# Value products of a block-local attention over two key blocks and three query blocks at a time, in a fused attention and feed-forward kernel

## The chip, the cores and the metric

One core of one Trainium2 chip runs the whole program. The metric is the device time of one execution in microseconds (us), as the median of several runs. Beside it stands one profiled execution, whose trace gives the start and the length of every instruction on TensorE (PE), VectorE (DVE), ScalarE (ACT) and GpSimd (POOL) and the issue of every DMA.

## The reference

```python
# q, k, v: (8 batches, 8 heads, 576, 64), float32
scores = np.matmul(q, k.transpose(0, 1, 3, 2)) / 8
rel = pos[:, None] - pos[None, :]
mask_local = (rel >= 0) & (rel < 32)                                # heads 0 to 3
mask_strided = (rel >= 0) & (pos[None, :] % 32 == pos[:, None] % 32)   # heads 4 to 7
attn = softmax(where(mask, scores, -1e9))
x = (attn @ v).transpose(0, 2, 1, 3).reshape(4608, 512)
h = x @ w_in                                                        # (4608, 2048)
g = where(h >= 1, h, where(h <= -1, 0, (h + 1) ** 2 / 4))
out = g @ w_out                                                     # (4608, 512)
```

A query of a local head sees itself and the 31 keys before it. With blocks of 32 positions, a query block needs its own key block and the one before: 64 keys.

## The kernel before, in words

The kernel does the attention batch by batch and the two products of the feed-forward block, which are most of the work, around it. The order is written out by hand: `AGENDA` is a list of times, each with the names of the steps that are recorded there. `2j0` is step `j` of unit 0 of batch 2. Engines run their own instructions in that order; DMAs are issued almost all on SP's queue, also in that order, and a DMA that waits holds all that stand behind it on the queue. DMA completions are counted on eight semaphores in turn, which SP's queue and the few DMAs on ACT's queue share: a DMA is issued only when the one before it on its semaphore has landed.

Each batch has four units. Unit 0 is the first twelve query blocks of the four local heads, unit 1 the other six, units 2 and 3 are the strided heads. The steps of unit 0 that matter here:

- `s`, score (line 592): for each query block, 32 queries against 64 keys, of two heads at a time (64 rows of the array each).
- `m` and the letters that follow: mask, softmax, in `pr`, 128 x 768.
- `t`, turn (line 743): DVE transposes 32 x 32 squares, into two tiles `t`.
- `j`, spread (line 753): two DMAs of 192 KB write them to a DRAM tile `there`.
- `J`, gather (line 764): four DMAs of 96 KB read them back into `pT`, so that the 64 keys of a query block stand on 64 partitions.
- `F`, fetch_v (line 538): loads of `v`, 384 KB for six query blocks; rows of a key block that two query blocks share stand there twice.
- `v`, value (line 779): for each of 12 query blocks and 4 heads one product, 64 keys x 64 columns of v as the stationary operand and 32 queries as the moving one. Four of them (two halves of the rows, two of the columns) fill the array.

A float32 product shows as two records in the trace, so the 48 products of unit 0 are 96 records of form `64*64 64x32`. Unit 1 and the strided units use the same line with 64x32 and 54x64.

The feed-forward block reads its weights as a stream: `wr<-kq` and `wr<-ks` (line 971, 256 KB each) go through a ring of seven tiles; every group of six matmuls (1.36 us) uses one up. These loads stand on SP's queue between the attention's DMAs. In the early part of the program the weights come in as `raw` (line 436) and are converted on ACT and POOL.

Of the kernel before, what the change touches and what calls it, by code (L numbers as in the profile page):

```python
# [8 lines left out]
F32 = mybir.dt.float32  # L9
# [25 lines left out]
-53.5 L3.1  # L35
-52.5 1s1 1m1 B3.1
-51.845 L7.1 A2.1 B2.1 D4.0 E4.0
# [42 lines left out]
0.95 2s0 D10 2m0 S10  # L80
2.51 2x0 2b0 2e0 2F1 2s1
4.5 C11 N11 2Q2 R11
5.45 2q0 2k0 2w0 2t0 2j0
6.51 D11 S11
# [22 lines left out]
31.45 3a2 2F2  # L107
33.45 3p1 S12 3w1 3t1 2V1 3j0 4Q0
35.45 3e2 2h1 3q2 2h3 3j1 C01
# [6 lines left out]
41.45 3J0  # L116
42.5 4m0 4x0 C02 3F1
43.45 3J1 3v0 N02 4s1 O00
# [11 lines left out]
59.45 4Q2 4s2 G0s10 G0t30 G0p60 4e1 4q1 R04 S03 3F2  # L130
59.95 3J3 4m2 S00 4j0 4p1 3V1 3h3 3h1
61.45 G0p32 4w1 4t1 4x2
63.45 G0s11
64.5 Y05 4F1 D04 4F0 4a2 4e2 4J0
65.45 4j1 N05
# [23 lines left out]
115 G0s40  # L159
117 S07 5F1 5e0 5q0 5k0 G0p41 G0s41 X1.1 X1.-6 X1.-4  # L160
119 R01 D01 G0s42
121 X1.6 G0s43 G0r30 S01 X1.7 X1.-5 G0r31
123 G0r40 5w0 5t0 X1.5 5m2 5x2 5b2
125.5 X1.4 G0r41 5j0 X1.3
128.5 5e2 5q2 5p2 5r2
131.5 5t2 5j2
# [14 lines left out]
163.5 5F2 6a1 5J1  # L181
170.5 6e1 6q1 6p1 6r1 6s2 6m2 6x2 6b2 5V1 6F1
171.5 6j0
175.5 6t1 6J0
179.5 G1s12
181 6F0
# [25 lines left out]
247.5 7w1  # L212
248.5 7F1
249.5 7a0 7e0
# [4 lines left out]
259.5 7q0 7k0 7r0  # L219
263.5 7t0 7j0  # L220
266.5 G2s11
267.5 G2p61
# [66 lines left out]
def tile_sparse_attention_then_ffn(  # L289
# [4 lines left out]
    v_l: bass.AP,  # L294
    v_s: bass.AP,
    w: bass.AP,
    out: bass.AP,
# [34 lines left out]
    def slots(u):  # L332

        n, rest = divmod(UNITS[u][2], IL if UNITS[u][0] else IS)
        return n + (rest > 0), n
# [50 lines left out]
    for i in range(IL):  # L386
        part = slice(i * QL, (i + 1) * QL)
        for n0, n1, off in ((0, SLOTS, ST),) if i else ((0, 1, 0), (1, SLOTS, ST)):
            t = m_loc[part, n0:n1]
            nc.gpsimd.affine_select(out=t, in_=t, compare_op=ALU.is_ge, fill=NEG, base=off,  # L390
                                    pattern=[[0, n1 - n0], [-1, WL]], channel_multiplier=1)
            nc.gpsimd.affine_select(out=t, in_=t, compare_op=ALU.is_ge, fill=NEG, base=ST - 1 - off,
                                    pattern=[[0, n1 - n0], [1, WL]], channel_multiplier=-1)
    for i in range(IS):
# [23 lines left out]
    SUMS_AT = (("X1a", "X1b", "w0", "w1", "w0", "w1", "w0", "w1"), ("X0b", "X0a", "X0b", "X0a", "w11", "w12", "w13", "w14"))  # L418
    w_v = w.bitcast(U32).rearrange("f p (i e t) -> f p i e t", i=2, t=2)

    kept = [[(dram.tile([P, 3, 2, HF], F32, tag=f"kq{i}{j}", name=f"kq_{i}_{j}"),
# [106 lines left out]
    def load_v(b, u, k=None):  # L528

        local, b0, nb = UNITS[u]  # L530
        if k is not None:
            b0, nb = b0 + k * VB, min(VB, nb - k * VB)
        src = (v_l if local else v_s)[b][:, b0:b0 + nb]
        if b == 0 and u in (0, 3):
            t = place(5 if u else 4, list(src.shape), F32, f"v_{b}_{u}")
        else:
            t = v_p.tile([P, VB, 2, D], F32, tag="v", name=f"v_{b}_{u}_{k}")[:, :nb]
        nc.sync.dma_start(t, src)
        for n in range(nb):
            loaded[b, local, b0 + n] = t[:, n]  # L540
# [6 lines left out]
    def fetch_v(b, *parts):  # L547
        for u, k in parts:
            if 0 < b < B and (b, UNITS[u][0], UNITS[u][1] + k * VB) not in loaded:
                load_v(b, u, k)  # L550


    def attention(b, kinds):

        probs, flipped, there, ahead, covered = {}, {}, {}, {}, set()
# [23 lines left out]
        def score(u, pairs=range(2)):  # L579
            local, b0, nb = UNITS[u]  # L580
            Q, W, I, p0 = (QL, WL, IL, 0) if local else (QS, WS, IS, 2)
            if 0 in pairs:
                probs[u] = banks(u, "s"), W
            sc = probs[u][0]
            for p in pairs:
                for n in range(nb):
                    q0 = (b0 + n) * (QL if local else WS)
                    k0 = max(q0 - ST, 0) if local else q0
                    for j in range(2):
                        _, s, i = seat(u, n, j)  # L590
                        qk = loaded[b, p0 + p, "qk"][j * D:(j + 1) * D]
                        nc.tensor.matmul(sc[j][i * Q:(i + 1) * Q, s, p], qk[:, 0, q0:q0 + Q],  # L592
                                         qk[:, 1, k0:k0 + W], start=u not in covered,
                                         stop=u not in covered)
# [23 lines left out]
        def homes(u):  # L618
# [15 lines left out]
            if ns[0] > ns[1]:  # L634
                todo += [(j, slice(j * 64, j * 64 + 64), ns[1], ns[0], ns[1]) for j in range(2)]
            pieces_ = []
            for j, part, s0, s1, at in todo:
                of = part, slice(2 * at, 2 * (at + s1 - s0))
                pieces_.append((sc[j][part, s0:s1], pr[of].rearrange("p (n h) w -> p n h w", h=2), part, of[1]))
# [107 lines left out]
        def spread(u):  # L747

            ts = probs.pop(u)
            n = sum(slots(u))  # L750
            there[u] = to = dram.tile([P, 2, 2, n, ST], F32, tag=f"t{u}", name=f"there_{b}_{u}")
            for h in range(2):
                nc.sync.dma_start(to[:, h], ts[h][:, :, :n])

        def gather(u):

            n = sum(slots(u))
            pool, tag = (o_p, "ob") if u == 1 else (pt_p, "pT")
            pT = pool.tile([P, 4, n if u == 1 else 2 * SLOTS, ST], F32, tag=tag, name=f"pT_{b}_{u}")
            src = there.pop(u).rearrange("(i c) h k n q -> h k c i (n q)", c=ST)  # L760
            for h in range(2):
                for k in range(2):
                    at = h * 64 + k * ST
                    nc.sync.dma_start(pT[at:at + ST, :, :n].rearrange("p i n q -> p i (n q)"), src[h, k])
            flipped[u] = pT

        def value(u, xp=None):
            local, b0, nb = UNITS[u]
            Q = QL if local else QS
            pT = flipped.pop(u)  # L770
            xp = xp or banks(u, "v")
            for n in range(nb):
                K = WL if local else LAST if b0 + n == NB_S - 1 else WS
# [389 lines left out]
    with tc.manual_schedule():  # L1163
# [25 lines left out]
        def step(name):  # L1189
# [12 lines left out]
            elif kind in "UV":  # L1202
                up(0, int(kind == "V"), rest == "0", rest == "1")
            elif kind == "W":
                for i in range(2):
# [67 lines left out]
def _layout(q, k, v, moe_w_in, moe_w_out):  # L1273
# [18 lines left out]
    keys = np.arange(0, S, QL)  # L1292
    keys = np.maximum(keys - ST, 0)[:, None] + np.arange(WL)[None, :]

# [3 lines left out]

    v_l = by_key(v[:, :HL][:, :, keys])
    v_s = np.pad(by_class(v[:, HL:]), [(0, 0)] * 2 + [(0, NB * WS - S), (0, 0)]).reshape(B, HL, NB, WS, D)  # L1300
    v_s = by_key(np.pad(v_s, [(0, 0)] * 3 + [(0, 64 - WS), (0, 0)]))
# [3 lines left out]
    w = np.concatenate([w_in, w_out.reshape(DFF // P, P, DM)], 2)  # L1305
    return {"qk_l": qk_l, "qk_s": qk_s, "v_l": v_l, "v_s": v_s, "w": w}

# [19 lines left out]
```

## Time and profile before

| | |
|---|---|
| median of 3 runs | 801.52 us (801.34 to 803.21) |
| the profiled execution | 802.56 us |
| its span, first to last instruction | 800.8 us |
| PE busy | 792.0 us, 99% of the span |
| DVE, ACT, POOL busy | 618.5, 505.2, 260.0 us |
| mean granted TensorE clock | 1.000 of full speed |
| moved by DMA | 209.78 MB, mean 262 GB/s |

The span is what the trace shows; the execution's own time is 1.76 us longer, and the median of the runs is 1.04 us below the profiled execution. In the trace's rows "x96" is a count of records merged into one row; the length of such a row reaches to the modelled end of the last one, which lies inside the next row, since matmuls are pipelined. In the chain of waits the pieces do not overlap.

### The profile page before, as it was taken

The numbers are of one execution on the slowest core, as the hardware profiler recorded it, in microseconds if no ns is written. First come the engines' busy times: TensorE is split into PE (matmuls) and PEld (weight loads), VectorE is DVE, ScalarE is ACT, GpSimd is POOL, SyncE is SP. The second block draws the span as 40 slices with busy tenths as digits, with TensorE's granted clock in tenths as the row PEclk, the third lists the DMA queues.
The fourth block names the chain that finished last, engine by engine and source line by source line (L and its number), as shares of the span: only waits on it lengthen the run. The fifth ranks groups of instructions, "written<-read, shape, count | busy, mean of one in ns | idle before, by whom it ended". The sixth has DMA issues, their size and how long they took to land.

```text
span 800.8 us, 17840 instructions
## 1 busy us (share of the span) xinstructions
PE 792.0 (99%) x6921; PEld 647.6 (81%) x6921; DVE 618.5 (77%) x881; ACT 505.2 (63%) x857; POOL 260.0 (32%) x203
## 2 busy tenths in 40 slices
PE   8999999999999999999999999999999999999998
PEld 6778888888887887878888888888888888888886
DVE  5999879989989999878689786675786854566673
ACT  5899854566764556677665456677544667775442
POOL 5456345887483320022141102132424001224000
PEclk9999999999999999999999999999999999999999
DMA  9948788898899999888889778777777675666665
GB/s 344 407 195 300 296 294 307 286 327 281 291 308 309 295 312 349 276 283 272 260 248 298 240 222 260 255 233 213 213 253 245 212 241 191 195 195 189 217 203 166
DMA packets 107699, 209.78 MB, mean 262 GB/s; under 512 B 17760, under 2 KB 33376, under 8 KB 105568
## 3 DMA queue, kind: packets, MB, share of 16 engines
q1 hardware_dynamic: 100560, 179.15, 69.5%
q10 hardware_dynamic: 7056, 29.49, 9.5%
q8 instruction: 55, 0.90, 0.5%
q14 instruction: 28, 0.23, 0.1%
HBM read 161.94 MB, written 46.66 MB: 260 GB/s over the span
## 4 chain that ended last, share of the span: by engine, by line
PE 95%; DMA 2%; issue 1%; DVE 1%; ACT 1%; POOL 0%; SPq 0%; POOLq 0%
PE yo L1135 21%; PE h L887 16%; PE y L1040 16%; PE zo L1135 11%; PE z L1040 8%; PE o L947 6%; PE xo L1135 5%; PE x L1040 4%; PE xp L779 3%; PE sc L592 3%; DMA qk<-in_qk_l 1%; DMA wr<-kq 1%; PE sc L577 0%; PE tp L719 0%; DVE xq_b L850 0%
## 5 line engine op out<-in xcount | busy, mean ns | idle before, releaser
L1135 PE MATMUL yo<-hl,wr 128*128 128x512 f32 x768 | 177.6, 390 | 0.0
L1135 PEld LDWEIGHTS yo<-hl,wr 128*128 128x128 f32 x768 | 143.5, 188 | 30.9 <-DVE hl L997 0.9
L1040 PE MATMUL y<-x,wr 128*128 128x512 f32 x576 | 139.9, 389 | 0.0
L1040 PEld LDWEIGHTS y<-x,wr 128*128 128x128 f32 x576 | 108.0, 188 | 22.5
L887 PE MATMUL h<-xq_a,w 128*128 128x512 f32 x384 | 122.9, 394 | 0.0
L1096 POOL TENSOR_TENSOR ga<-gb,ga 128x1024 f32<-128x1024 f32 x17 | 44.1, 2601 | 236.3 <-DVE ga L897 175.5
L997 DVE TENSOR_TENSOR hl<-ga,hl 128x1024 fp32r<-128x1024 f32 x48 | 63.9, 1346 | 36.6 <-ACT hl L996 35.0
L1135 PE MATMUL zo<-hl,wr 128*128 128x512 f32 x384 | 89.4, 391 | 0.0
L887 PEld LDWEIGHTS h<-xq_a,w 128*128 128x128 f32 x384 | 72.0, 188 | 15.7
L1135 PEld LDWEIGHTS zo<-hl,wr 128*128 128x128 f32 x384 | 71.6, 188 | 15.8 <-DVE hl L997 0.6
L996 ACT CAST hl<-ga 128x1024 fp32r<-128x1024 f32 x48 | 50.0, 1052 | 51.1 <-PE yo L1135 16.3
L887 PE MATMUL h<-xq_b,w 128*128 128x512 f32 x192 | 73.6, 391 | 0.1
L1040 PE MATMUL z<-x,wr 128*128 128x512 f32 x288 | 73.5, 390 | 0.0
L1040 PEld LDWEIGHTS z<-x,wr 128*128 128x128 f32 x288 | 53.8, 188 | 11.3
L894 ACT ACTIVATE tmp<-tmp 128x512 f32<-128x512 f32 x96 | 60.9, 634 | 3.1
L997 DVE TENSOR_TENSOR hl<-gb,hl 128x1024 fp32r<-128x1024 f32 x36 | 48.7, 1367 | 14.4 <-ACT hl L996 14.3
L996 ACT CAST hl<-gb 128x1024 fp32r<-128x1024 f32 x36 | 37.8, 1057 | 31.2 <-PE zo L1135 15.2
L504 POOL TENSOR_TENSOR st<-st 128x256 f32<-128x256 f32 x48 | 50.7, 1059 | 14.0 <-DVE st L705 6.4
L897 DVE SCALAR_TENSOR_TENSOR ga<-ga,tmp 128x512 f32<-128x512 f32 x48 | 33.1, 689 | 28.3 <-ACT tmp L894 28.0
L891 ACT ACTIVATE u<-h,half 128x512 f32<-128x512 f32 x48 | 32.9, 686 | 30.2 <-PE h L887 21.2
L469 POOL TENSOR_TENSOR raw<-raw 128x512 uint32<-128x512 uint32 (+1 forms) x34 | 35.9, 1067 | 42.1 <-DVE raw L465 16.7
L682 POOL TENSOR_TENSOR pr<-pr,st 128x384 f32<-128x384 f32 (+3 forms) x18 | 26.7, 1487 | 63.8 <-DVE st L678 63.7
(124 smaller groups left out, 1409.1 us busy)
## 6 DMA issues: line engine op xcount, KB each, us to landing
wr<-ks SPq DMA_DIRECT2D x224, 256.0 KB, 4.0
wr<-kq SPq DMA_DIRECT2D x168, 256.0 KB, 3.4
ks<-st ACTq DMA_DIRECT2D x16, 1024.0 KB, 7.0
raw<-in_w SPq DMA_DIRECT2D x30, 512.0 KB, 9.7
qk<-in_qk_s SPq DMA_DIRECT2D x16, 604.0 KB, 6.9
qk<-in_qk_l SPq DMA_DIRECT2D x16, 576.0 KB, 6.7
kq<-w ACTq DMA_DIRECT2D x16, 512.0 KB, 3.8
v<-in_v_l SPq DMA_DIRECT2D x21, 384.0 KB, 5.5
```

The costliest lines, as they stand in the source:

```text
L469: nc.gpsimd.tensor_tensor(out=raw[:, :, 1], in0=raw[:, :, 1], in1=raw[:, :, 0], op=ALU.add)
L504: eng.tensor_tensor(out=st[:, to, 1], in0=st[:, x, 1], in1=st[:, y, 1], op=op)
L887: nc.tensor.matmul(o_ps[c, f], weight(f, 0, h)[:, x, e:e + P], xq[c][y][:, cc], start=first and n == 0, stop=last and n == len(todo) - 1)
L891: nc.scalar.activation(u, h, AF.Relu, bias=half, scale=0.5)
L894: nc.scalar.activation(u, u, AF.Square)
L897: nc.vector.scalar_tensor_tensor(out=to, in0=h, scalar=1.0, in1=u, op0=ALU.max, op1=ALU.min)
L947: nc.tensor.matmul(o_ps["o"][d], weight(f, 1, h)[:, x, e:e + P], gs[y], start=f == 0 and n == 0, stop=f == NF - 1 and n == 2)
L996: nc.scalar.copy(t[:, 0], src)
L997: nc.vector.tensor_tensor(out=t[:, 1], in0=src, in1=t[:, 0].bitcast(F32), op=ALU.subtract)
L1040: nc.tensor.matmul(to, w_[:, a, c * P:(c + 1) * P], xc[m][:, b, c], start=m in (1, 2, 5) and c + q == 0, stop=c == 1 and q == 2, skip_grou ...
L1096: eng.tensor_tensor(out=to, in0=x, in1=y, op=op)
L1135: nc.tensor.matmul(to, w_[jj][:, a, d * P:(d + 1) * P], t[:, b, jj], start=m in (1, 2, 5) and k + jj + q == 0, stop=k == NP // 2 - 1 and j ...
```

## The change

From batch 2 on, unit 0 goes another way. Its twelve query blocks see the keys of twelve blocks (and the one before the first, which does not exist). A product now takes two neighbouring key blocks as the stationary operand, 64 rows of v with no row twice, and as the moving operand the three query blocks that see any of them, 96 columns; the sums of neighbouring products overlap by one query block and are accumulated. A query block that sees only one of the two key blocks needs zeros for the other. They come from DRAM: a tile `windows` lies there for the whole program, is filled with zeros where needed by a new step `Z` (one memset on POOL, five DMAs), and each batch writes its turned probabilities between the zeros.

Per batch this makes 24 products (20 with 96 columns, 4 with 64) of 48 (with 32); one v load of 384 KB of two; twelve small write DMAs (16 to 48 KB each) of two; two gathers of 128 x 576 (288 KB) of four of 32x4x192 (96 KB). The second gathered tile stands in a buffer of the v pool. In the agenda the write step stands twice, one call for each half; for batches 5, 6 and 7 the halves stand apart, with two weight loads between. Batches 0 and 1 keep the old way. The mask is built with fewer operations, and the score step reads its keys 32 positions further left for the first block, where the mask hides them.

```diff
--52.5 1s1 1m1 B3.1
+-52.5 Z 1s1 1m1 B3.1
...
-59.95 3J3 4m2 S00 4j0 4p1 3V1 3h3 3h1
+59.95 3J3 4m2 S00 4j0 4j0 4p1 3V1 3h3 3h1
-64.5 Y05 4F1 D04 4F0 4a2 4e2 4J0
+64.5 Y05 D04 4F0 4a2 4e2 4J0
...
 125.5 X1.4 G0r41 5j0 X1.3
+127.5 5j0
...
+    windows = dram.tile([2, 2, ST, 36, ST], F32, tag="windows", name="windows")
+
+    def empty_windows():
+
+        t = o_p.tile([ST, 2, 6 * ST], F32, tag="ob", name="empty")
+        nc.gpsimd.memset(t, 0.0)
+        for h in range(2):
+            for r in range(2):
+                to = windows[h, r].rearrange("c (i x) q -> c i (x q)", i=2)
+                nc.sync.dma_start(to[:, :, :6 * ST] if r else to[:, :, 12 * ST:], t)
+        nc.sync.dma_start(windows[:, 1, :, 34:].rearrange("h c n q -> c h (n q)"), t[:, :, :2 * ST])
...
+        if b > 1 and u == 0:
+            t = loaded[b, "v_w"] = v_p.tile([P, VB, 2, D], F32, tag="v", name=f"v_{b}_w")
+            nc.sync.dma_start(t, v_w[b])
+            return
...
     def attention(b, kinds):
+
+        def wide(u):
+
+            return b > 1 and u == 0
...
+            if wide(u):
+                h = 2 - len(ts)
+                t = ts.pop(0)
+                if ts:
+                    probs[u] = ts
+                for i in range(4):
+                    odd, second = divmod(i, 2)
+                    of, to = t[i * ST:(i + 1) * ST].rearrange("c k n q -> c k (n q)"), windows[h, :, :, second * 3 * n:]
+                    if odd:
+                        nc.sync.dma_start(to[:, :, n:2 * n].rearrange("k c n q -> c k (n q)"), of)
+                        continue
+                    nc.sync.dma_start(to[0, :, :n].rearrange("c n q -> c (n q)"), of[:, 1])
+                    before = windows[h, 1, :, (5 - 3 * second) * n:(5 - 3 * second) * n + n - 2 + 2 * second]
+                    nc.sync.dma_start(before.rearrange("c n q -> c (n q)"), of[:, 0, (2 - 2 * second) * ST:])
+                return
...
+            if wide(u):
+                src = windows.rearrange("h r c (i x) q -> i (h r c) (x q)", i=2)
+                flipped[u] = []
+                for i, (pool, tag) in enumerate(((pt_p, "pT"), (v_p, "v"))):
+                    t = pool.tile([P, 3, n, ST], F32, tag=tag, name=f"pT_{b}_{u}_{i}")
+                    nc.sync.dma_start(t.rearrange("p g n q -> p (g n q)"), src[i])
+                    flipped[u].append(t)
+                return
...
+            if wide(u):
+                for n in range(nb // 2):
+                    m = min(3, nb - 2 * n)
+                    for p in range(2):
+                        for j in range(2):
+                            keys = slice(p * 64, p * 64 + 64)
+                            nc.tensor.matmul(xp[p][j * D:(j + 1) * D, 2 * n:2 * n + m], loaded[b, "v_w"][keys, n, j],
+                                             pT[n % 2][keys, :m, n // 2 * 2 + j], start=n == 0, stop=n == nb // 2 - 1,
+                                             skip_group_check=True)
```

On PE, the value products of unit 0 of batch 4 begin so before the change; `xp_0_0` and `xp_0_1` are the PSUM tiles of the two halves of the rows, "x2" is the two halves of the columns, and the piece repeats to 24 such rows:

```order
L779 MATMUL xp_0_0_3506<-pT_0_3451,v_0_0_3447 64x32 x2
L779 MATMUL xp_0_1_3507<-pT_0_3451,v_0_0_3447 64x32 x2
...
L779 MATMUL xp_0_0_3506<-pT_0_3451,v_0_1_3444 64x32 x2
L779 MATMUL xp_0_1_3507<-pT_0_3451,v_0_1_3444 64x32 x2
```

and with the change all of it is twelve rows, the two gathered tiles taken in turn:

```order
L831 MATMUL xp_0_0_3479<-pT_0_0_3425,v_w 64x96 x2
L831 MATMUL xp_0_1_3480<-pT_0_0_3425,v_w 64x96 x2
L831 MATMUL xp_0_0_3479<-pT_0_1_3427,v_w 64x96 x2
L831 MATMUL xp_0_1_3480<-pT_0_1_3427,v_w 64x96 x2
...
L831 MATMUL xp_0_0_3479<-pT_0_1_3427,v_w 64x64 x2
L831 MATMUL xp_0_1_3480<-pT_0_1_3427,v_w 64x64 x2
```

Half as many instructions of three times the columns stand in the same place, behind the same scores and ahead of the same `yo` products.

On SP's queue, before the change, the spread and the gather of unit 0 of batch 4 stand so (`there_0` and `pT_0` are theirs; the `wr` loads between are of the feed-forward stream, `pT_3` is another unit's):

```order
L764 DMA pT_3_3306<-there_3_3139 32x4x160 x4
L753 DMA there_0_3317<-t_0_0_3219 128x384
L753 DMA there_0_3317<-t_0_1_3221 128x384
L971 DMA wr_3377<-kq_0_169 128x512
L971 DMA wr_3404<-kq_1_171 128x512
L971 DMA wr_3427<-kq_2_173 128x512
L538 DMA v_0_1_3444<-in_v_l 128x768
L538 DMA v_0_0_3447<-in_v_l 128x768
L764 DMA pT_0_3451<-there_0_3317 32x4x192 x4
L753 DMA there_1_3457<-t_1_0_3396 128x2x96
```

and with the change (the second half's six writes read like the first's, of `t_0_1`):

```order
L817 DMA pT_3_3273<-there_3_3106 32x4x160 x4
L792 DMA windows<-t_0_0_3186 32x192
L794 DMA windows<-t_0_0_3186 32x128
L792 DMA windows<-t_0_0_3186 32x192
L794 DMA windows<-t_0_0_3186 32x192
L790 DMA windows<-t_0_0_3186 32x2x192 x2
...
L1035 DMA wr_3353<-kq_0_165 128x512
L1035 DMA wr_3380<-kq_1_167 128x512
L1035 DMA wr_3403<-kq_2_169 128x512
L547 DMA v_w<-in_v_w 128x768
L808 DMA pT_0_0_3425<-windows 128x576
L808 DMA pT_0_1_3427<-windows 128x576
```

Three weight loads, the v load and the gather now stand behind twelve writes in place of two.

The new step `Z` stands early on the same queue, where before four `raw` loads and two `qk` loads followed each other:

```order
L450 DMA raw_748<-in_w 128x1024 x2
L450 DMA raw_783<-in_w 128x1024 x2
L432 DMA windows<-empty 64x1x192 x4
L433 DMA windows<-empty 32x2x64
L450 DMA raw_943<-in_w 128x1024 x2
L450 DMA raw_986<-in_w 128x1024 x2
L539 DMA qk_2_1047<-in_qk_s 128x1208
```

Its five DMAs wait for the memset on POOL, and the loads behind them wait with them.

## Rows read from the trace of the kernel before

**Rows 1.** The page: PE's busy time, and the chain that ended last by engine.
```profile
PE 792.0 (99%) x6921; PEld 647.6 (81%) x6921; DVE 618.5 (77%) x881; ACT 505.2 (63%) x857; POOL 260.0 (32%) x203
...
PE 95%; DMA 2%; issue 1%; DVE 1%; ACT 1%; POOL 0%; SPq 0%; POOLq 0%
```

**Rows 2.** Chain of waits at three value products: start us, us, what, records.
```profile
81.75 0.83 PE xp L779 x48
...
144.58 1.53 PE xp L779 x96
...
268.27 0.86 PE xp L779 x48
```

**Rows 3.** Tile xp, windows 144 to 147 and 598 to 600: ns min/median/max, starts, form.
```profile
L779 PE MATMUL xp<-pT,v x96: 219/219/240, 144.5 to 145.9; 64*64 64x32 f32 x96
...
L779 PE MATMUL xp<-pT,v x48: 218/218/267, 598.4 to 599.1; 54*64 54x64 f32 x48
```

**Rows 4.** Timeline of PE at two groups of local scores: start us, us.
```profile
185.76 1.17 PE L592 MATMUL sc<-qk 64*32 64x64 f32 x96
...
194.07 0.77 PE L592 MATMUL sc<-qk 64*32 64x64 f32 x48
```

**Rows 5.** DMA issues of the page: count, KB each, median us to landing.
```profile
raw<-in_w SPq DMA_DIRECT2D x30, 512.0 KB, 9.7
...
there<-t SPq DMA_DIRECT2D x24, 192.0 KB, 3.6
```

**Rows 6.** Timeline of SP's queue, 214 to 246 us: start, us in which they were issued.
```profile
215.16 0.81 SPq L753 DMA_DIRECT2D there<-t  x2
...
219.51 1.59 SPq L538 DMA_DIRECT2D v<-in_v_l  x2
221.21 5.45 SPq L764 DMA_DIRECT2D pT<-there  x4
```

**Rows 7.** Line 764, 221 to 233 us: ns of an issue, first and last start; landing.
```profile
L764 SPq DMA_DIRECT2D pT<-there x4: 779/1264/1689, 221.2 to 225.9; - x4
...
DMA to landing us min/median/max: 5.0/6.6/8.6
```

**Rows 8.** Timeline of PE, 230 to 236 us, batch 4's value products and what follows.
```profile
231.80 1.73 PE L779 MATMUL xp<-pT,v 64*64 64x32 f32 x95
233.46 2.79 PE L1135 MATMUL yo<-hl,wr 128*128 128x512 f32 x11
```

**Rows 9.** Waits of SP's queue, 214 to 232 us: us in total, times, longest.
```profile
SPq L764 <- DMA ks<-st: 1.7, 1, 1.7
```

**Rows 10.** Line 764, 134 to 147 us, batch 2: issues and landing.
```profile
L764 SPq DMA_DIRECT2D pT<-there x4: 423/936/1834, 135.3 to 139.2; - x4
...
DMA to landing us min/median/max: 2.2/2.8/4.7
```

**Rows 11.** Timeline of SP's queue, 312 to 352 us: the gather of batch 5.
```profile
333.28 1.85 SPq L764 DMA_DIRECT2D pT<-there  x4
```

**Rows 12.** Timeline of PE, 336 to 352 us: batch 5's value products, a wait behind them.
```profile
339.82 1.65 PE L779 MATMUL xp<-pT,v 64*64 64x32 f32 x96
...
349.85 0.72 PE L592 MATMUL sc<-qk 64*32 64x64 f32 x48 [0.49 <-DMA qk<-in_qk_l]
```

**Rows 13.** Chain of waits, 339 to 352 us.
```profile
340.77 9.03 DMA qk<-in_qk_l
```

**Rows 14.** Timeline of SP's queue, 30 to 56 us.
```profile
30.27 6.28 SPq L436 DMA_DIRECT2D raw<-in_w  x6
```

**Rows 15.** Timeline of POOL, 30 to 50 us.
```profile
38.50 2.15 POOL L469 TENSOR_TENSOR raw<-raw 128x512 uint32<-128x512 uint32 x2 [1.45 <-DVE raw L465]
```

**Rows 16.** Timeline of ACT, 44 to 56 us.
```profile
52.64 0.71 ACT L457 ACTIVATE raw<-raw 128x512 f32<-128x512 f32 x1
```

**Rows 17.** Timeline of PE, 46 to 60 us, scores of batch 1's strided heads.
```profile
55.65 0.92 PE L592 MATMUL sc<-qk 64*64 64x54 f32 x48
```

**Rows 18.** DMA between 40 and 56 us, in 40 equal slices of the window.
```profile
GB/s 379 430 399 440 369 420 379 410 405 435 401 396 433 408 403 421 326 290 290 157 97 60 24 0 0 0 0 0 0 0 0 0 0 0 0 0 0 0 0 0
```

## The prediction before the run

> **What bounds the kernel now.** I read the page first: PE is busy for 792.0 of 800.8 us, and the chain that ended last is 95% PE [rows 1]. So a saving counts when it shortens PE's own list of instructions, and it stays only if nothing that PE waits for was already due at the moment of its need. The reader should therefore look for two things: what the value products cost in PE's chain, and how early their operands land.
>
> In the chain, 96 records of the 64x32 form take 1.53 us, 48 of them 0.83 us [rows 2]. The difference is 0.70 us for 48 records, 14.6 ns each, or 58 ns for a round of four that fills the array; 0.13 us is fixed. The form with 64 moving columns takes 0.86 us for 48 [rows 2]: twice the columns cost 0.03 us once, and nothing per round. The durations say the same: the first record is 240 ns long with 32 columns and 267 with 64, 0.84 ns for each column, while the others have 219 and 218 [rows 3]. So up to 64 columns a round has its floor of 58 ns in something other than the columns, which I take to be the loading of four 64-column stationary blocks.
>
> **The change part by part.**
>
> *Fewer products.* Per batch 24 rounds of 32 columns become 10 rounds of 96 and 2 of 64. No row shows 96 columns on 64 stationary ones. The nearest price is that of the first record: 96 x 0.84 = 81 ns, above the floor, so the columns would now set the round. Then 10 x 81 + 2 x 58 = 0.93 us, and the fixed part 0.13 + 2 x 0.027 = 0.18 us: 1.11 us, 0.42 less than 1.53. One bound is the floor again: 12 x 58 + 180 = 0.88 us, a saving of 0.65. The other comes from the scores, where stationary blocks of 32 columns leave the columns as the limit: (1.17 - 0.77) / 48 = 8.3 ns a record [rows 4], eight to fill the array, 67 ns for 64 columns, 100 for 96: 1.30 us, a saving of 0.23. I take 0.42, since the first-record price is measured on the same instruction. Six batches: 2.5 us, bounds 1.4 and 3.9.
>
> A rule of the Trainium skill speaks against this. "TensorE: Matmul & The Clock Gate", Part 3, The mechanism, says that a weight load overlaps with running matmuls only where they use other rows of the array. Here two column blocks share their rows, and by that rule load and columns would add. The 64-column form contradicts it so far, for there the columns would have to show in each round, and they don't. I keep it as a rival.
>
> *Batch 5's share.* Right after the value products of batch 5 come scores that wait for a `qk` load [rows 12]; it was issued at 340.77 and took 9.03 us in the chain [rows 13]. Its issue follows SP's queue, not these products, so PE would reach the wait 0.42 us sooner and wait 0.42 us longer. I count nothing for batch 5: 5 x 0.42 = 2.1 us.
>
> *Twelve writes for two.* SP issues a DMA in about 0.41 us (0.81 for two [rows 6]). Twelve take 4.9 us, 4.1 more. The gather has two issues fewer and the v load one: about 1.3 us back. Whether the rest matters depends on how early the gather lands:
> - Batch 2: last issue at 139.2 and 2.2 to 4.7 us to landing [rows 10], products at 144.58 [rows 2]: about 3 us to spare, against 4.1 - 1.3 = 2.8. Batch 3 stands alike, batches 6 and 7 have far more.
> - Batch 4: last issue at 225.9, then at least 5.0 us [rows 7], 230.9, products at 231.80 [rows 8]: less than 1 us to spare. But here the queue did not run free. The gather waited 1.7 us for a `ks` store on its completion semaphore [rows 9], and v loads and gather spread over 219.51 to 226.66 [rows 6]. Twelve writes from 215.1 end at 220, the three `wr` loads and one v load at 222; the extra issues fill time in which the queue stood, and the gather can again be out by about 226. It also has about 200 KB less ahead of it or in it (384 less of v, 192 more of its own), 0.5 us at the 400 GB/s of [rows 18]. After the savings of batches 2 and 3 PE wants it 0.84 us sooner, at 231.0. I charge 0.3 us of waiting.
> - Batch 5: issue ends at 335.13 [rows 11], products start at 339.82 [rows 12], so nothing to spare; but the writes are issued twelve us before, and a wait here is taken from that for `qk`. Nothing.
>
> *The stream.* In batches 5 to 7 six writes at a time (2.5 us) stand between weight loads. PE uses one load in 1.36 us from a ring of seven, so a load is issued up to 8.2 us ahead; I take them as hidden, with up to 1 us as the other bound.
>
> *The step Z.* Its DMAs wait for a memset that POOL reaches after 40.65 [rows 15]. The memset has 384 elements a partition where a step there has 512 and takes 1.08 us, which I take as its upper bound. Five issues later, at 43.8, the four `raw` loads follow, before within 30.27 to 36.55 [rows 14]. 2 MB at about 400 GB/s [rows 18] land by 49 to 50; ACT takes the last at 52.64 [rows 16]. The two `qk` loads behind (1.2 MB) land by 53, wanted at 55.65 [rows 17]. The median 9.7 us of `raw` [rows 5] is that of a full queue; [rows 18] shows an idle one from 49 us on. Nothing, with 1 us as the other bound.
>
> *The rest.* DVE and ACT keep their instructions; POOL has two mask operations fewer at the start. Neither is on the chain. The DMA volume falls by about 200 KB a batch.
>
> **The sum.** -2.1 + 0.3 = -1.8 us against the profiled execution: 802.56 - 1.8 = 800.8; the median lies 1.04 below that execution, so 799.7 us.
>
> **The rivals.**
> - *B, all of it pays.* The wait for `qk` in batch 5 (0.49 us) shrinks since less is moved, batch 4 does not wait, and the slower groups go too: batch 4's last records and products took 1.66 us from 231.80 to 233.46, batch 5's similar. Then 6 x 0.42 + 0.5 + 0.2 = 3.2 us, or up to 3.9 if 96 columns stay near the floor: 798.2. For it: DMAs end the last waits of [rows 9, 12], and they get lighter. Against: they also get more numerous.
> - *C, load and columns add* (the skill's rule above, as a mechanism): a round is 58 + 81 = 139 ns, twelve with the fixed part 1.85 us, 0.3 more than now, 5 x 0.3 + 0.3 = +1.8: 803.3. The 64-column rows speak against it.
> - *D, the gather of batch 4 is late* and the change ends slower. If all 2.8 us of extra issue delay it, it is out at 228.7 and lands at 233.7, with PE ready at 231.0: 2.7 us, and the `yo` products behind have weight loads that queue after it, bound by the same delay. At batch 2 the same 2.8 us just use up what is spare. Net -2.1 + 2.7 = +0.6: 802.1; with 1 us each from the stream and Z, 804. It decides at a landing after 233.1. For it: the twelve writes take their turn on the completion semaphores as well, and one that comes behind a 1 MB `ks` store holds everything. And twelve writes must land where two took 3.6 us [rows 5]. The Trainium skill states a rule with the same sense ("DMA: Bandwidth & Descriptors", Bandwidth): transfers under 64 KB are dominated by their descriptors, and these are 16 to 48 KB; how late that makes them here no row shows.
>
> **How the numbers follow.** What a measurement here can tell from no change is about 0.3%, 2.4 us: faster means below 799.1, slower above 803.9. Forecast (798.8 to 800.6) 0.42, B 0.25, C 0.05, D 0.28. Faster: B and a fifth of the forecast's, 0.34. Slower: the upper part of D and a little of C, 0.14. The rest, 0.52, is no difference. The range reaches from B's end (3.9 us below 801.5, with 0.4 us for the median itself) to C and most of D: 797.2 to 803.6.
>
> **What would show it.** Right: records of the 64x96 form at 1.1 us a batch in the chain (0.9 or 1.3 at the bounds; 1.85 is rival C), a wait of `sc` for `qk` near 350 us of 0.9 us, and hardly a wait of the value products for a DMA. Wrong: a wait of `xp` for `pT` near 231 us above 1 us, waits of `yo`, `xo` or `zo` for `wr` behind the writes of batches 5 to 7, or ACT waiting for `raw` near 52 us.

## The result: slower by 1.2%

The changed kernel takes 811.71 us (median of 6 runs, 809.34 to 812.71) against 801.52 for the kernel before: a ratio of 1.0119, 95% interval 1.0101 to 1.0137. It lies outside the predicted range (797.2 to 803.6), on the side of rival D. The profiled execution has a span of 810.7 us, 9.9 more than before.

The page of the changed kernel, PE's busy time and the chain by engine, beside [rows 1]:

```profile
PE 793.0 (98%) x6633; PEld 647.1 (80%) x6633; DVE 618.7 (76%) x881; ACT 504.0 (62%) x857; POOL 257.7 (32%) x203
...
PE 88%; DMA 5%; DVE 3%; SPq 1%; issue 1%; ACT 1%; POOL 1%; DVEq 0%; POOLq 0%
```

PE has 288 records fewer and yet is busy 1 us longer. Its share of the chain has fallen from 95% to 88%; DMAs, VectorE and SP's queue hold 9% of it, before 3%. The products are not to blame. The chain at batch 3's value products (start us, us, records):

```profile
201.93 1.10 PE xp L831 x48
```

1.10 us in place of the 1.53 of [rows 2]. What was gained there is lost elsewhere. The waits of PE in the changed kernel (us in total, times, longest):

```profile
PE h L951 <- DVE xq_b L914: 3.4, 1, 3.4
PE xp L831 <- DMA pT<-windows: 1.7, 3, 1.2
PE xp L831 <- ACT u L955: 1.5, 1, 1.5
PE yo L1199 <- DMA wr<-kq: 1.3, 1, 1.3
PE sc L619 <- DMA qk<-in_qk_l: 1.3, 2, 0.7
```

The feed-forward matmuls of 128x512 are the same in both kernels and in the same order, so the start of the same one in both traces tells where the time went (us):

| behind what | before | after | later by |
|---|---|---|---|
| start of the first ones, at a low clock in the trace after | 56.5 | 57.6 | 1.1 |
| scores of batch 2 | 136.1 | 137.6 | 1.4 |
| value products of batch 2 | 146.0 | 148.9 | 2.9 |
| next scores, which need a `qk` load | 153.3 | 157.1 | 3.7 |
| the wait for `xq_b` | 182.5 | 189.9 | 7.4 |
| the low clock behind it | 185.4 | 194.7 | 9.3 |
| value products of batch 3 | 194.8 | 203.7 | 8.9 |
| value products of batch 4 | 233.5 | 244.1 | 10.6 |
| a wait for a `wr` load | 308.4 | 320.0 | 11.6 |
| value products of batch 5 | 341.4 | 352.3 | 10.9 |
| the `qk` wait of [rows 12] | 350.5 | 360.5 | 10.0 |
| value products of batches 6 and 7 | 576.4 | 586.3 | 9.9 |

Nearly all is lost between 137 and 244 us, at batches 2, 3 and 4, and the largest single piece is the wait for `xq_b`.

The part of batch 2 does not begin with the writes. Ahead of them VectorE normalizes the probabilities, and in this trace that operation takes 3.10 us in place of 0.96: POOL began an operation of its own 0.11 us before it, and VectorE's ends 0.8 us behind POOL's. So the first write starts at 133.14 us, against 129.88 before the change; 1.1 us of this lateness is older. The timelines of VectorE and POOL, first in the changed kernel, then in later_turns, a kernel below whose order differs from the change only from batch 3 on:

```profile
129.30 2.39 POOL L513 TENSOR_TENSOR st<-w 128x1024 f32<-128x1024 f32 x1 [1.66 <-DMA ks<-st]
129.41 3.10 DVE L736 TENSOR_TENSOR pr<-pr,st 128x768 f32<-128x768 f32 x1
...
130.14 0.96 DVE L736 TENSOR_TENSOR pr<-pr,st 128x768 f32<-128x768 f32 x1
130.18 3.19 POOL L513 TENSOR_TENSOR st<-w 128x1024 f32<-128x1024 f32 x1 [1.79 <-DVE st L735]
```

In the fourteen traces of this case VectorE's operation takes 0.96 us where it began first (ten), and 3.1 to 3.2 where POOL did, by at most 0.14 us (four: the change, later_turn, ten_more and ten_later). In later_turns the twelve writes cost batch 2 nothing: PE is 1.89 us late ahead of its products and 1.46 behind them, less by the 0.43 that the products save. So the 2.6 us that the changed kernel's trace loses between 136 and 157 us need this turn of events besides the writes. How often the runs without a trace had it is not on record.

VectorE's timeline at batch 3 (start us, us, idle before and who ended it):

```profile
182.29 0.38 DVE L773 STREAM_TRANSPOSE t<-pr 128x192 f32<-128x192 f32 x1
187.77 0.38 DVE L773 STREAM_TRANSPOSE t<-pr 128x192 f32<-128x192 f32 x1 [5.10 <-DMA windows<-t]
188.07 0.65 DVE L961 SCALAR_TENSOR_TENSOR g<-h,u 128x512 f32<-128x512 f32 x1
...
189.37 0.89 DVE L914 TENSOR_TENSOR xq_b<-xp,xq_a 128x144 fp32r<-128x144 f32 x4
```

The transpose is the turn of unit 1. Its output goes into one of the three buffers that hold turned tiles, and the one it gets is still being read by the small writes of unit 0. VectorE stands 5.10 us before it, with `g` and `xq_b` queued behind, and PE waits for these. The chain shows that a write had it for 5.80 us, and PE's timeline the other end of the wait, at the matmul that needs `xq_b`:

```profile
181.84 5.80 DMA windows<-t
```

PE's timeline:

```profile
189.91 0.91 PE L951 MATMUL h<-xq_b,w 128*128 128x512 f32 x2 [3.39 <-DVE xq_b L914]
```

The writes that VectorE waited for are the 48 KB ones of the second half. They were issued at 181.37 and 181.84 us, right behind a store of 1 MB on ACT's queue, and landed 0.2 and 0.4 us after that store, which took 6.0 us:

```profile
181.28 0.34 ACTq L529 DMA_DIRECT2D ks<-st  x1
```

The same stands at batches 2 and 4: there the two writes behind such a store took 4.7 and 4.2 to 4.5 us to land, the store 4.6 and 4.5. Of the 36 writes of batches 2 to 4, the 19 that were issued while a `ks` store was on its way took 0.69 us to issue and 3.9 to land in the median, the other 17 took 0.42 and 1.7. Before the change the two writes of batch 4, at 215.16, were out ahead of the store and landed in 1.9 us. A longer row of writes runs into the next store; no run took the stores away, so how much of the price is theirs is not shown.

Stretches of the trace (PE, PEld, DVE, ACT, POOL busy, then the granted clock): PE's clock is down behind the idle time at batch 3, and it is down near 25 us.

```profile
24.00:28.00 4.00, 4.00 (x55) 3.31 (x48) 3.41 (x12) 3.05 (x13) 0.93 (x1) 0.57 1.03 413
189.00:195.00 6.00, 5.09 (x14) 3.65 (x14) 5.92 (x15) 2.25 (x3) 2.24 (x3) 0.72 0.82 241
```

A mean of 0.72 means that part of the stretch ran at 1.2 GHz in place of 2.4; by the table it cost 1.9 us on top of the wait. Near 25 us no such idle time stands before it: PE was idle for 1.00 us before 23.6, and the trace of two_writes has the same 1.00 us there and a full clock.

SP's queue at batch 4, beside [rows 6]:

```profile
223.87 0.31 SPq L792 DMA_DIRECT2D windows<-t  x1
224.23 1.53 SPq L794 DMA_DIRECT2D windows<-t  x1
...
227.74 1.16 SPq L792 DMA_DIRECT2D windows<-t  x1
228.94 0.96 SPq L794 DMA_DIRECT2D windows<-t  x1
229.95 0.85 SPq L792 DMA_DIRECT2D windows<-t  x1
230.85 1.22 SPq L794 DMA_DIRECT2D windows<-t  x1
232.11 0.90 SPq L790 DMA_DIRECT2D windows<-t  x2
233.05 2.55 SPq L1035 DMA_DIRECT2D wr<-kq  x3
...
236.79 1.22 SPq L808 DMA_DIRECT2D pT<-windows  x2
```

Twelve writes take from 223.87 to 233.01, 9.1 us, where two took 0.81. Some are issued in 0.3 to 0.45 us each, others hold the queue for 0.85 to 1.53 us. The gather is out at 238.0; its second DMA, issued at 237.6, lands 5.5 us later, at 243.1. PE reached the products at 241.0, and its timeline shows the wait, one of the prediction's signs of being wrong, in two parts, the first of which the trace puts down to an instruction of ACT that came last by the profile:

```profile
242.45 0.51 PE L831 MATMUL xp<-pT,v_w 64*64 64x96 f32 x8 [1.48 <-ACT u L955]
243.11 1.00 PE L831 MATMUL xp<-pT,v_w 64*64 64x96 f32 x40 [0.16 <-DMA pT<-windows]
```

### The profile page after: what moved, and what is told of

Its sections match the earlier page's. It is cut to its first block, busy times and chain, and to the rows that moved or that the text cites. A ratio compares the mean times of both kernels' runs of the same rounds, so it can differ in the third digit from the quotient of the medians.

```text
span 810.7 us, 17322 instructions
## 1 busy us (share of the span) xinstructions
PE 793.0 (98%) x6633; PEld 647.1 (80%) x6633; DVE 618.7 (76%) x881; ACT 504.0 (62%) x857; POOL 257.7 (32%) x203
## 4 chain that ended last, share of the span: by engine, by line
PE 88%; DMA 5%; DVE 3%; SPq 1%; issue 1%; ACT 1%; POOL 1%; DVEq 0%; POOLq 0%
PE yo L1199 21%; PE y L1104 16%; PE h L951 13%; PE zo L1199 10%; PE z L1104 8%; PE xo L1199 5%; PE o L1011 4%; PE x L1104 4%; PE sc L619 2%; PE xp L843 2%; DMA qk<-in_qk_l 2%; DMA wr<-kq 1%; DMA v<-in_v_l 1%; DMA windows<-t 1%; DMA pT<-windows 1%
## 5 line engine op out<-in xcount | busy, mean ns | idle before, releaser
L951 PE MATMUL h<-xq_a,w 128*128 128x512 f32 x384 | 125.0, 400 | 0.2 <-DVE g L961 0.2
```

The costliest lines, as they stand in the source:

```text
L951: nc.tensor.matmul(o_ps[c, f], weight(f, 0, h)[:, x, e:e + P], xq[c][y][:, cc], start=first and n == 0, stop=last and n == len(todo) - 1)
```

## The experiments

Each ratio is to the kernel before on the same chip, with its 95% interval.

| kernel | ratio | interval |
|---|---|---|
| five_more | 0.9977 | 0.9964 to 0.9990 |
| ten_tiny | 0.9982 | 0.9964 to 1.0000 |
| two_writes | 0.9990 | 0.9978 to 1.0002 |
| mask_score | 0.9999 | 0.9985 to 1.0012 |
| ten_more | 1.0047 | 1.0027 to 1.0067 |
| later_turns | 1.0068 | 1.0043 to 1.0093 |
| later_turn | 1.0080 | 1.0054 to 1.0107 |
| the change | 1.0119 | 1.0101 to 1.0137 |
| pool_queue | 1.0175 | 1.0130 to 1.0220 |
| ten_later | 1.0188 | 1.0152 to 1.0223 |
| ten_writes | 1.0208 | 1.0169 to 1.0246 |
| split_writes | 1.0260 | 1.0233 to 1.0287 |
| act_queue | 1.0440 | 1.0411 to 1.0469 |

**The writes undone, the rest kept**

```diff
-                for i in range(4):
-                    ...
+                to = windows[h].rearrange("r c n q -> (r c n q)")[:P * 2 * n * ST].rearrange("(p x) -> p x", p=P)
+                nc.sync.dma_start(to, t[:, :, :n].rearrange("p k n q -> p (k n q)"))
```

> The changed kernel, but each half of the probabilities goes to DRAM as one contiguous DMA of 192 KB (two a batch, as before the change) in place of six small ones, so the values of unit 0 from batch 2 on are computed from a wrong layout; the zero fill covers all of the DRAM tile. Gather, v load and products are those of the change. Theory 1 (the twelve writes hold SP's queue and the turned tiles): the waits of batches 2 to 4 and the 5.1 us wait of DVE for the writes go, and the products' saving of 2.1 to 2.5 us shows: 799 to 802 us, with at most 1.2 us of that the slow start near 25 us. Theory 2 (the gather of two large DMAs and its buffer in the v pool make the loads late): the time stays at 808 to 812.

801.05 us. With two large writes, which leave out the layout between the zeros, all waits of batches 2 to 4 are gone, with the large gathers, the buffer in the v pool and the new products still there. So it is the twelve writes, at batch 2 together with the long operation of VectorE, which this trace has not. Of the saving 0.1% shows, and the interval reaches past 1. The trace tells what became of batch 5's share: the chain has the same `qk` load that [rows 13] show, and PE's timeline has two waits for such loads, 0.92 us together, where [rows 12] have 0.49: longer by what the products saved.

```profile
339.92 8.97 DMA qk<-in_qk_l
...
347.62 0.82 PE L618 MATMUL sc<-qk 64*32 64x64 f32 x48 [0.43 <-DMA qk<-in_qk_l]
348.94 0.73 PE L618 MATMUL sc<-qk 64*32 64x64 f32 x48 [0.49 <-DMA qk<-in_qk_l]
```

**The writes done alone**

```diff
             for h in range(2):
+                if b > 1 and u == 0:
+                    for i in range(4):
+                        part = slice(i * ST, (i + 1) * ST)
+                        for k in (slice(0, 2),) if i % 2 else (slice(1, 2), slice(0, 1)):
+                            nc.sync.dma_start(to[part, h, k], ts[h][part, k, :n])
+                    continue
                 nc.sync.dma_start(to[:, h], ts[h][:, :, :n])
```

> The kernel before, with one part of the change alone: from batch 2 on the write of unit 0's probabilities is twelve DMAs of 24 and 48 KB in place of two of 192 KB, same place and same bytes in DRAM; products, gather, v loads and agenda as before. Theory 1: the waits come with the writes alone: 808 to 813 us, with a DVE wait for the writes near 182 us and PE waiting behind it. Theory 2: 801 to 802.5.

824.13 us, above the 808 to 813 expected and more than twice the change's loss. VectorE waits for the writes as in the change, at batches 3 and 4 (us in total, times, longest):

```profile
DVE t L743 <- DMA there<-t: 7.9, 2, 4.9
```

Batch 2 loses nothing here: VectorE's operation takes 0.96 us in this trace. The excess comes from batch 4 on (13.9 us late behind it, 10.3 in the change) and above all at batches 5 and 7. There the change puts its halves apart with weight loads between, while here all twelve stand in a row, and between 308.7 and 331.8 and again between 440 and 535 us the same matmuls slip by another 3.9 and 3.5 us. That the row does it is likely and not taken apart: the trace puts PE's longest waits there down to VectorE's turn (2.1 us) and to ACT (3.3). This kernel is that of before up to batch 2, and its trace, too, has a low clock between 24 and 28 us:

```profile
24.00:28.00 4.00, 3.85 (x63) 3.17 (x64) 3.09 (x9) 2.40 (x11) 1.04 (x1) 0.63 1.04 416
```

So the 1.1 us that the changed kernel's trace loses there can come without the change, and two_writes, which shares its program up to the first writes but for the form of the zero fill, has a full clock there.

**One stall taken away by order**

```diff
-33.45 3p1 S12 3w1 3t1 2V1 3j0 3j0 4Q0
-35.45 3e2 2h1 3q2 2h3 3j1 C01
-35.95 2l3
+33.45 3p1 S12 3w1 2V1 3j0 3j0 4Q0
+35.45 3e2 2h1 3q2 2h3 C01
+35.95 2l3 3t1 3j1
```

> The changed kernel, with the turn and the write of batch 3's unit 1 moved a little later in the order, behind the conversions of xp to xq_b that TensorE waits for. Theory 1 (DVE stood 5.1 us in front of that turn, for buffers that the small writes still read, and PE 3.4 us behind it, and then ran 1.9 us longer at the low clock): that stall goes, about 5.3 us less, 805.5 to 808 us, and no low clock near 190 us. Rival (the same lateness shows at the next thing that batch 3 needs, the gather): 809 to 812.

809.14 us, in the rival's range. The matmul at 185.4 us of the kernel before is 3.7 us late in place of 9.3, as theory 1 had it. Half of it is given back at batch 4, where VectorE's timeline now has the same wait, which it did not have there in the changed kernel:

```profile
232.78 0.38 DVE L773 STREAM_TRANSPOSE t<-pr 128x192 f32<-128x192 f32 x1 [2.05 <-DMA windows<-t]
```

PE's timeline just behind it:

```profile
234.52 0.50 PE L951 MATMUL h<-xq_a,w 128*128 128x512 f32 x1 [2.08 <-DVE g L961]
```

**The mask and the key window alone** (with the keys of `v_l`, and none of the diff's other hunks)

```diff
-                    k0 = max(q0 - ST, 0) if local else q0
+                    k0 = qk_of.shape[2] + (q0 - ST if local else q0)
...
+    nc.gpsimd.memset(m_loc[:QL, 0, :ST], NEG)
```

> The kernel before, with the new mask and the new key window of the score step alone; products, writes and gathers as before. If these are what makes PE's clock fall near 25 us (1.2 us lost there in the changed kernel): about 802.7 us and a low clock between 24 and 28 us. Rival (the fall comes from elsewhere in the change): 801 to 802 and full clock.

802.12 us against 802.15: they cost nothing and bring nothing, and the clock is full between 24 and 28 us.

**A full queue without held buffers**

```diff
                 nc.sync.dma_start(to, t[:, :, :n].rearrange("p k n q -> p (k n q)"))
+                for i in range(5):
+                    nc.sync.dma_start(spare[h * 5 + i], ident[:ST])
```

> The kernel of two_writes (801.05 us, values from a wrong layout) with ten more DMAs a batch on SP's queue, five behind each half's write: 16 KB each, from a constant tile to a place in DRAM that nobody reads. The queue is as full as in the change, but no buffer that VectorE waits for hangs on the ten. If the place on the queue and its completion semaphores are the cost: the late gathers and qk loads of batches 2 to 4 come back, 804 to 807 us, without a wait of DVE for buffers near 182 us. If the buffers held by the small writes are all of it: 801 to 802.

806.64 us, a ratio 0.0057 above that of two_writes: about half of the change's loss, and no wait of VectorE for buffers. The late gathers come back: PE waits 2.9 us in all for `pT<-windows`, part of it at batch 2, where this trace has VectorE's long operation too.

**The same on other queues** (all twelve writes moved; act_queue with `nc.scalar`)

```diff
-                        nc.sync.dma_start(to[:, :, n:2 * n].rearrange("k c n q -> c k (n q)"), of)
+                        nc.gpsimd.dma_start(to[:, :, n:2 * n].rearrange("k c n q -> c k (n q)"), of)
...
```

> The changed kernel, with the twelve writes of a batch issued on POOL's queue in place of SP's. If SP's queue is the cost (issues and shared completion semaphores): the late gathers and loads go, the buffers come free sooner too, and 799.5 to 802 us are left. If the small writes land late on whatever queue: DVE still waits for them near 182 us and 806 to 811 us remain. POOL has to issue them (its price is not in a trace here), and its own work on st and pr can be late: up to 3 us more.

818.12 us, more than either case expected. At batch 2 nothing is lost: the matmul behind the products is 0.3 us early (0.15 ahead of them), not 2.9 late. But on POOL the writes of the later batches stand behind that engine's own work, 9.35 us of it at batch 3, and VectorE waits more than twice as long for them. POOL's timeline:

```profile
169.47 9.35 POOL L518 TENSOR_TENSOR st<-st 128x256 f32<-128x256 f32 x8
```

The waits of VectorE (us in total, times, longest):

```profile
DVE t L773 <- DMA windows<-t: 11.1, 3, 5.4
```

> The changed kernel, with the twelve writes of a batch issued on ACT's queue. An issue there takes 0.33 to 0.36 us, twelve 4.2 us of an engine that TensorE waits for at once, and they share SP's completion semaphores. If it is only SP's place on the queue that costs: 800 to 803 us. If an issue that waits holds whatever engine it stands on: 806 to 815.

838.41 us, beyond both ranges. ACT starts no work of its own for up to 10.5 us at a time. The list of waits puts it down to the writes:

```profile
ACT st L727 <- DMA windows<-t: 10.5, 1, 10.5
```

In these 10.5 us, before 242.9, ACT issues the twelve writes, which begin at 232.19, and in the middle of the row it waits 2.4 us for a `ks` store on its completion semaphore. Issues, and the waits among them, hold the engine that they stand on; on SP they hold only other DMAs.

**Both stalls moved** (on top of later_turn's edit)

```diff
-61.45 G0p32 4w1 4t1 4x2
+61.45 G0p32 4w1 4x2
-64.5 Y05 D04 4F0 4a2 4e2 4J0
+64.5 Y05 D04 4F0 4a2 4e2 4J0 4t1
```

> The changed kernel, with the turn and write of unit 1 moved later in the order for batch 3 (as in later_turn) and for batch 4 too, so that VectorE does work that TensorE needs first. If the stall of VectorE for buffers held by the small writes is worth the difference between the changed kernel (811.71) and ten_more (806.64): 804.5 to 807.5, no wait of DVE for the writes over 1 us. If the stall only moves on once more: 808.5 to 811.

808.29 us: between the two expectations, and its interval overlaps that of later_turn. VectorE's wait is down to 1.8 us, but PE waits 3.8 us for `pT<-windows` (1.7 in the change), part of it at batch 5, which had no such wait. In both kernels, what order takes from one wait is in part due again at the next thing that hangs on the writes.

**Five more, and ten tiny ones** (ten_more with `range(2 + h)`; ten_more with 512 bytes: `spare[h * 5 + i, :1], ident[:1]`)

> As ten_more, with five more DMAs of 16 KB a batch in place of ten (two behind the first half's write, three behind the second's). If every issue on SP's queue costs alike: half of ten_more's 5.6 us over two_writes, 803.2 to 804.5. If the queue has room up to a point (3 us to spare at batch 2, and so on): 800.8 to 802.5.

801.45 us, ratio 0.9977: the price is not proportional. Seven writes a batch cost nothing, the twelve of ten_more do.

> As ten_more, but each of the ten extra DMAs is 512 bytes of one partition in place of 16 KB of 32, so that it lands at once. If the time of issuing them is what the queue costs (10 x 0.42 us a batch): as ten_more, a ratio near 1.0047. If it is their landing (eight completion semaphores for twelve DMAs, each held until the DMA has landed): as five_more and two_writes, 0.9975 to 0.9995.

801.33 us, ratio 0.9982. As many issues as in ten_more, and no cost. SP's queue at batch 4 in ten_more:

```profile
218.66 0.34 SPq L788 DMA_DIRECT2D windows<-t  x1
219.05 4.31 SPq L790 DMA_DIRECT2D spare<-ident  x5
223.46 0.95 SPq L788 DMA_DIRECT2D windows<-t  x1
224.46 3.79 SPq L790 DMA_DIRECT2D spare<-ident  x5
...
231.94 1.24 SPq L804 DMA_DIRECT2D pT<-windows  x2
```

and in ten_tiny:

```profile
215.00 0.33 SPq L788 DMA_DIRECT2D windows<-t  x1
215.38 1.45 SPq L790 DMA_DIRECT2D spare<-ident  x5
216.93 0.35 SPq L788 DMA_DIRECT2D windows<-t  x1
217.37 4.84 SPq L790 DMA_DIRECT2D spare<-ident  x5
...
224.93 1.18 SPq L804 DMA_DIRECT2D pT<-windows  x2
```

Five tiny ones are issued in 1.45 us when nothing holds them (0.29 each); five of 16 KB take 4.31, of which one takes 1.83. (The 4.84 hold 3.5 us of waiting for a `ks` store.) From the first write to the first issue of the gather it is 13.3 us in ten_more (231.94 - 218.66), 9.9 in ten_tiny, and 6.1 in the kernel before [rows 6], whose four gather issues then took 5.45 where ten_tiny's two take 1.18. So the gather is out 11.5 us behind the first write before and 11.1 in ten_tiny, but 14.5 in ten_more.

The completion semaphores are not what holds the writes at batch 4. A wait for one shows in the list of SP's waits, as in the change at batch 3, where one write waits for a `ks` store; between 222 and 239 us, the whole row of batch 4, that list has no DMA (us in total, times, longest):

```profile
SPq L792 <- DMA ks<-st: 2.4, 1, 2.4
...
SPq L792 <- DVE t L773: 2.7, 1, 2.7
SPq L808 <- PE h L951: 0.7, 1, 0.7
SPq L798 <- DVE hl L1061: 0.2, 1, 0.2
```

Nor has that of ten_more between 217 and 233 us. The issues themselves are long.

**Fewer, wider writes**

```diff
-                for i in range(4):
-                    ...
+                of = t.rearrange("p k n q -> p k (n q)")
+                to = windows[h].rearrange("r c (s x) q -> s c r (x q)", s=2)
+                nc.sync.dma_start(to[:, :, 0, :n * ST], of[:64, 1])
+                for k in range(2):
+                    nc.sync.dma_start(to[:, :, k, n * ST:2 * n * ST], of[64:, k])
+                ...
```

> The best that I can make of the change with its right output: the order of later_turns, and ten writes a batch in place of twelve (three of them of 48 KB over 64 partitions in each half). Against later_turns it has two issues fewer in each of six batches: if those cost what ten cost in ten_more (0.56 us each over all batches), 1.1 us less than later_turns, 803.5 to 806.5. If only the stall mattered, the same as later_turns. Faster than the kernel before (802) only if the queue's part is gone too, which I do not expect.

This one has later_turns' order too. 817.92 us, a miss (803.5 to 806.5 expected). ten_writes has the wider writes in the order of the change, so that the two effects come apart:

> The changed kernel with the ten writes of ten_later and its own order: what made ten_later slow. If the form of the writes (64 partitions in two groups of 32, 48 KB) is slow to land: slower than the changed kernel, a ratio above 1.014, with longer waits of DVE for buffers. If the moved steps did it: 1.008 to 1.012.

819.33 us, so the order is not what failed. Three of five writes of a half now carry 48 KB from 64 partitions to two groups of rows. VectorE waits longest of all for them:

```profile
DVE t L773 <- DMA windows<-t: 13.1, 3, 6.7
```

So fewer issues do not help. By VectorE's waits these writes land later than the twelve; the trace gives no landing time of this form, so neither that nor its cause is shown directly. No version that puts the probabilities between the zeros beats the kernel before.

## Why the prediction was wrong

*Right.* The products: 1.11 us foretold, 1.10 in the chain, and rival C's 1.85 is excluded; the rule of the Trainium skill ("TensorE: Matmul & The Clock Gate", Part 3, The mechanism), by which loads and columns of blocks in the same rows would add, does not hold for these blocks; the same section excepts loads into a background weight buffer, which no run here tells apart. Batch 5's share is lost to the `qk` load, as foretold, in the trace of two_writes; ten_tiny's and the change's own have no wait there. Mask and score cost nothing (mask_score); batches 5 to 7 lose nothing to the writes where these stand in halves. Batch 2's slack, "about 3 us to spare" against 2.8, was enough where VectorE's operation was short (later_turns). With the writes out of the way the forecast comes close: the spans of ten_tiny and two_writes are 798.8 and 799.3 us, 2.0 and 1.5 below the 800.8 of before, where 1.8 was foretold. By the ratios of all their runs it is 1.4 and 0.8 us, and neither interval is clear of 1.

*Wrong: "Twelve writes for two".* Three steps of it failed.
- I took 0.41 us for an issue, from two DMAs on a queue with room, and found 4.1 us for ten more. At batch 4 it was 8.3 (9.1 against 0.81). ten_tiny shows that the count alone does not cost; five_more and ten_more, that five writes of 16 KB more cost nothing and ten do.
- "The extra issues fill time in which the queue stood" is refuted there: the writes themselves were slow to issue, up to 1.53 us each, and the gather was out 14.1 us behind the first write (238.01 - 223.87), against 11.5 [rows 6]. The term of 0.3 us of waiting was 1.6 (1.48 and 0.16), in a kernel already nine us late.
- I asked when the gather lands and not who waits for the writes to land. The turned tiles are free only then, VectorE's next turn wants one, and PE wants what stands behind that turn on VectorE. This is 5.3 of the 9.9 us, and no rival of mine has it. Rival D was the right direction by half of its mechanism, priced at +0.6 to +2.5 and given 0.28. Its "two took 3.6 us" is the median of all 24 writes of 192 KB; at batch 4 the two took 1.9. (Rival B's sum, 3.2 us less, gives 798.3 and not 798.2, which changes nothing.)

*The parts.* By the ratios, two_writes to ten_more is 0.57% (4.6 us) without a held buffer, and ten_more to the change another 0.72% (5.8 us), which is about the 5.3 of the stall at batch 3 with its low clock. The split is rough: ten_more writes 544 KB a batch where the change writes 368, its trace has VectorE's long operation at batch 2, and the stall undone by order gave back 0.39% in later_turn and 0.51% in later_turns, not all of it. That the writes cause both is shown by two_writes and split_writes, from either side. Of the 9.9 us of the trace, the 1.1 near 25 us and the long operation ahead of batch 2 are not theirs.

*Z* was priced at nothing; in the change's trace it shows no wait, while in that of later_turns PE waits 2.0 us for the early `qk` loads that stand behind it, more than the other bound of 1 us. Whether `Z` is the cause there is not shown.

*What stays open.* What makes an issue long where no semaphore holds it, and how much of it and of the late landing is due to the `ks` stores on their way: ten_tiny takes away bytes and pieces alike. Why VectorE waits longest in ten_writes. And the wait for `wr` near 308 us (1.3 us), which the trace of the change has and those of two_writes, ten_more and later_turn have not.

## What to carry to other kernels

A DMA out of a buffer has two prices: its place on the queue, and the time until the buffer is free. Before splitting a write, list who allocates that buffer next and what is queued behind that instruction on its engine, for there the landing time is paid, on an engine that the DMA has nothing to do with. An issue time read from a queue with room is no price for a dozen in a row: look at the slack of each place, and at what other transfers will be on their way by then. And compare several traces before a loss is put down to the change: here 0.1 us in the order of two engines moved 2 us.

## What was not expected of the hardware

- Of two operations on VectorE and POOL that begin within 0.35 us of each other, the later one takes longer: VectorE's 3.1 us in place of 0.96, POOL's about 3 in place of 2.4.
- Five DMAs of 512 bytes are issued in 1.45 us, five of 16 KB at the same place in 4.31.
- Writes of an eighth of the size (24 KB) took 2.6 us to land in the median, far from an eighth of the 3.6 of 192 KB [rows 5]. The DMA issues of the changed kernel's trace (count, KB each, median us to landing):

```profile
windows<-t SPq DMA_DIRECT2D x24, 48.0 KB, 2.0
windows<-t SPq DMA_DIRECT2D x36, 24.0 KB, 2.6
windows<-t SPq DMA_DIRECT2D x12, 16.0 KB, 2.6
```

  The Trainium skill's rule ("DMA: Bandwidth & Descriptors", Bandwidth), that transfers under 64 KB are dominated by their descriptors, agrees with these rows in so far as the time does not follow the size; I named it for rival D and took no price from it.
- A round of four products takes as long with 64 moving columns as with 32 (58 ns), and the ten rounds of 96 with two of 64 take 1.10 us: by the fixed part and the floor of the prediction, (1.10 - 0.18 - 2 x 0.058) / 10 = 80 ns each. What sets the floor of 58 ns no run took apart.
- PE idle for 3.4 us cost 1.9 us more at the low clock. It was low near 25 us too, in five of the fourteen traces (means of 0.57 to 0.67 from 24 to 28 us), among them split_writes, whose program up to there is that of the kernel before.
